# Three-column shift tiles, a new split of the weight turns, an earlier first projection tile and projection steps in the drain of an attention + feed-forward kernel

## Chip, cores, metric

One core of one Trainium2 chip. The metric is device microseconds (us) of one execution. Each kernel ran several times in turn with the kernel before ("timed"); one of these runs of each kernel was profiled and left the trace. Each kernel has one trace, so a position in a trace is one execution's.

## The reference

```
q, k, v: [8 batches, 8 heads, 576 rows, 64]    w_in: [512, 2048]   w_out: [2048, 512]
scores = q k^T / 8;  keep scores >= rowmax - tau (0.02), others get weight 0
attn   = exp(scores - rowmax) / sum;  x = attn v        # x: 4608 rows x 512
out    = (h - tanh(h)) @ w_out,  h = x @ w_in
```

## The kernel before

It works in slots: slot s does the score matmuls of query tile s+8, its own weights and the attention matmuls of tile s-2. There are 32 head pairs of 9 query tiles: 4 "A" tiles, each followed by a "B" tile of the same head, and a middle tile "M" with both heads' last 64 rows, in position 4. Four pairs are a batch. Beside attention in batch m run the hidden steps (h) of block m-1 and the projection steps (y, four quarters for each of four row tiles) of block m-2, one step being four 512-column matmuls on TensorE. VectorE makes `g` = h - tanh(h); `yo` is the copy of a finished y tile out of PSUM. The drain is what follows the slot of the last query tile.

A score tile leaves PSUM by a VectorE copy that also takes the row maximum (`sc`, `mx`). One more small VectorE operation makes the bias `nb = tau - max` of an A and a B tile together (the shift). ScalarE bends (`z`), the tile is turned (on TensorE into `psZ`, or by the DMA crossbar into `zT`), ScalarE takes exp (`pT`), TensorE multiplies with v. GpSimd splits the next pair's k and q into two fp16 parts and copies a swapped k (`kS`).

```python
def on_pe(i):                       # which tiles are turned on TensorE
    p, j = divmod(i, TPP)
    return p < HPAIR or p < 2 * HPAIR and j in (0, 1, 4, 5, 6)
...
    if kind(j) == "B":              # in scores(i)
        mx = mxs[i] = mxs.pop(i - 1)
    else:
        mx = mxs[i] = st_pool.tile([P, 2], F32, name="mx", tag="mx")
    c = int(kind(j) == "B")
    nc.vector.tensor_scalar(
        out=sc, in0=ps[:, lo : lo + S], scalar1=SC, scalar2=None,
        op0=ALU.mult, op1=ALU.max, accum_out=mx[:, c : c + 1])
...
def shift(i):                       # called one slot after scores(i)
    kd = kind(i % TPP)
    if kd == "A":
        return
    n = 2 if kd == "B" else 1
    mx = mxs.pop(i)
    nb = st_pool.tile([P, 2], F32, name="nb", tag="nb")
    nc.vector.tensor_scalar(
        out=nb[:, 0:n], in0=mx[:, 0:n], scalar1=-1.0, scalar2=tau,
        op0=ALU.mult, op1=ALU.add)
    nbs[i] = nb[:, n - 1 : n]
    if kd == "B":
        nbs[i - 1] = nb[:, 0:1]
...
EARLY = lambda m: 3 if m else 0     # quarters of y(m,0) done in the stage of h(m)
...
for s in range(-AHEAD, NTILE + LAG + 3):       # main loop, cut
    ...shift(s + 7); scores(s + 8); kink(s + 5)
    weights(s)                                  # turn on TensorE if on_pe, exp
    ...one step of todo (h or y)...
    attend(s - LAG); norm; emit_x(pair that is done)   # emit_x: psX, then VectorE copies xT, xR
    ...loads, splits (GpSimd), turns of k and q...
while stage < NMB:                  # the last two stages, after the loop
    for step in layers(stage, True): ...
```

The first h step of a stage reads all four pairs' x, the last of which `emit_x` has just turned: its fourth matmul needs VectorE's copy `xT`, and in the trace before it waited for it once from 126 to 463 us, for 0.5 us.

Of the kernel before, what the change touches and what calls it, by code (L numbers as in the profile page):

```python
# [9 lines left out]
F32 = mybir.dt.float32  # L10
# [8 lines left out]
def kernel(  # L19
# [11 lines left out]
    nc = tc.nc  # L31
# [22 lines left out]

    def on_pe(i):
        p, j = divmod(i, TPP)
        return p < HPAIR or p < 2 * HPAIR and j in (0, 1, 4, 5, 6)

    W = 2 * S

# [34 lines left out]
    for i in range(NM):  # L95
        zm = const.tile([P, 5 * P], BF16, name=f"zm{i}")
        nc.vector.memset(zm[:, S : 5 * P], -STEEP)
        zms.append(zm)


    own = const.tile([P, 2, D], BF16, name="own")
    nc.vector.memset(own, 0.0)
# [127 lines left out]

    def q_by_dma(p):

        return p >= 2 * HPAIR and p % 2 == 1

    def turn(p, t):
        hl = hls.pop((p, t))
# [52 lines left out]
    def scores(i):  # L289
        p, j = divmod(i, TPP)  # L290
        qT, kT, kS = mats[p, "q"], mats[p, "k"], mats[p, "ks"]
        ps = ps_big.tile([P, 1024], F32, name="psS", tag="big")
        main, rem, lo = slice(0, 512), slice(512, 576), 0
        if kind(j) == "B":
            main, rem, lo = slice(512, 1024), slice(448, 512), 448
        if j == 4:
            qrem = REM
            if q_by_dma(p):
                qrem = (slice(512, 640, 2), slice(513, 640, 2))
            for n, kk in enumerate((kT, kS)):  # L300
                for dst, srcs in ((main, MAIN), (rem, REM)):
                    for hh in range(2):
                        nc.tensor.matmul(  # L303
                            out=ps[64 * hh : 64 * hh + 64, dst],
                            lhsT=qT[:, qrem[hh]], rhs=kk[:, srcs[hh]],
                            start=(n == 0), stop=(n == 1),
                        )
        else:
            hh = int(j > 4)
            lhs = qT[:, j * P : (j + 1) * P]  # L310
            for n, kk in enumerate((kT, kS)):
                for dst, src in ((main, MAIN[hh]), (rem, REM[hh])):
                    nc.tensor.matmul(  # L313
                        out=ps[:, dst], lhsT=lhs, rhs=kk[:, src],
                        start=(n == 0), stop=(n == 1),
                    )
        sc = sc_pool.tile([P, S], F32, name="sc")
        if kind(j) == "B":
            mx = mxs[i] = mxs.pop(i - 1)
        else:  # L320
            mx = mxs[i] = st_pool.tile([P, 2], F32, name="mx", tag="mx")
        c = int(kind(j) == "B")
        nc.vector.tensor_scalar(  # L323
            out=sc, in0=ps[:, lo : lo + S], scalar1=SC, scalar2=None,
            op0=ALU.mult, op1=ALU.max, accum_out=mx[:, c : c + 1],
        )
        scs[i] = sc

    def shift(i):

        kd = kind(i % TPP)
        if kd == "A":
            return
        n = 2 if kd == "B" else 1
        mx = mxs.pop(i)
        nb = st_pool.tile([P, 2], F32, name="nb", tag="nb")
        nc.vector.tensor_scalar(  # L337
            out=nb[:, 0:n], in0=mx[:, 0:n], scalar1=-1.0, scalar2=tau,
            op0=ALU.mult, op1=ALU.add,
        )  # L340
        nbs[i] = nb[:, n - 1 : n]
        if kd == "B":
            nbs[i - 1] = nb[:, 0:1]

# [142 lines left out]
    def bend():  # L487
        while halves:
            m, n, ps = halves.pop(0)
            th = t_pool.tile([P, MB], F32, name="th")  # L490
            nc.scalar.activation(out=th, in_=ps, func=ACT.Tanh)  # L491
            ths.append((m, n, ps, th))

    def shrink():
        while ths:
            m, n, ps, th = ths.pop(0)
            nc.vector.scalar_tensor_tensor(  # L497
                out=gs[m][:, n, :], in0=th, scalar=-1.0, in1=ps,
                op0=ALU.mult, op1=ALU.add,
            )  # L500
# [26 lines left out]
                    )  # L527


    EARLY = lambda m: 3 if m else 0  # L530
    LAST = 1
    quarters = lambda m: [(m, ms, part) for ms in range(4) for part in range(4)]

    def layers(m, tail):


        def h_step(n):
            if tail and n % 2:
                ps = ps_big.tile([P, MB], F32, name="psHt", tag="big")
            else:  # L540
                ps = ps_h.tile([P, MB], F32, name="psH", tag="h")
            hidden(m, n, ps)

        def y_step(m, ms, part):
            if part == 0:
                odd = ms % 2
                pl, tag = (ps_o, "o") if tail and odd else (ps_y, "y")
                ys[m, ms] = pl.tile([P, d_model], F32, name="psY", tag=tag), odd
            ps, odd = ys[m, ms]
            project(m, ms, part, ps, tail and odd)  # L550

        def y_half(h):

            n = d_model // 2
            pl, tag = ((ps_y, "y"), (ps_o, "o"))[1 - h]
            ps = pl.tile([P, n], F32, name="psY", tag=tag)
            for part in range(4):
                project(m, 3, part, ps, h == 0, slice(h * n, h * n + n))

        now = quarters(m - 1)[EARLY(m - 1) :] if m > 0 else []  # L560
        if m < NMB - 1:
            now += quarters(m)[: EARLY(m)]
        else:
            now += quarters(m)[:12]
        n = 16 + len(now)


        ahead = n - max(0, EARLY(m) - 3) - LAST if m < NMB - 1 else n - 9 - LAST
        steps, at, i = [], [], 0

        def ready(y):
            last = 4 * y[2] + 3
            return y[0] < m or len(at) > last and at[last] + 2 < i

        while now or len(at) < 16:
            if len(at) < 16 and (
                not now or not ready(now[0]) or len(at) * ahead <= i * 16
            ):
                steps.append(lambda a=len(at): h_step(a))
                at.append(i)  # L580
            elif ready(now[0]):
                steps.append(lambda y=now.pop(0): y_step(*y))
            else:
                steps.append(lambda: None)
            i += 1
        if m == NMB - 1:
            steps += [lambda h=h: y_half(h) for h in range(2)]
        return steps
# [68 lines left out]
        if at < -AHEAD:  # L657
            plan.setdefault(-AHEAD, []).extend(plan.pop(at))

    kinks = {}  # L660
    for i in range(NTILE):
        kinks.setdefault(i // 2 * 2 + 2 - AHEAD if i < 4 else i - MASK, []).append(i)
    for s in range(-AHEAD, NTILE + LAG + 3):
        p, j = divmod(max(s, 0), TPP)
        if 0 <= s < NTILE and j == 2 + LAG and p % HPAIR == 0 and p >= HPAIR:
            assert not todo
            todo = layers(stage, False)
            share = len(todo) / (HPAIR * TPP - 2 - LAG)
            done, stage = 0.0, stage + 1
        if 0 <= s + AHEAD - 1 < NTILE:  # L670
            shift(s + AHEAD - 1)
        if 0 <= s + AHEAD < NTILE:
            scores(s + AHEAD)
        if s == 1 - AHEAD:
            for t in ("k", "q", "ks"):
                turn_first(t, 1)
        for i in kinks.pop(s, []):
            kink(i)
        bend()
        if 0 <= s < NTILE:  # L680
            weights(s)
            if todo:
                done += share
                if j == TPP - 1 and p % HPAIR == HPAIR - 1:
                    done = 1e9
                while todo and done >= 1:
                    todo.pop(0)()
                    done -= 1
        if s == 0:
            nc.vector.tensor_tensor(  # L690
                out=fold, in0=ident_bf[:, 0:64], in1=ident_bf[:, 64:P], op=ALU.add
            )
        shrink()
        for store in stores[:-1]:
            store()
        del stores[:-1]
        if 0 <= s - LAG < NTILE:
            attend(s - LAG)
            pp, jj = divmod(s - LAG, TPP)
            if jj == 4:  # L700
                norm(pp, 0)
            if jj == 8:
                norm(pp, 1)
        pp, jj = divmod(s - LAG, TPP)
        if jj == 1 and 0 < pp <= NPAIR:
            emit_x(pp - 1)
        for step in plan.pop(s, []):
            step()
        if True:
            if s + AHEAD in w_when:  # L710
                if loaded:
                    w_cast()
                piece = next(pieces, None)
                if piece:
                    w_load(piece)

    while stage < NMB:
        for step in layers(stage, True):
            step()
            bend()  # L720
            shrink()
            for store in stores:
                store()
            stores.clear()
        stage += 1
# [37 lines left out]
```

## Time and profile before

| | before |
|---|---|
| timed, median of 6 runs in the comparison with the change | 544.65 us (544.19 to 545.59) |
| span of the profiled run | 542.9 us |
| busy TensorE, VectorE, ScalarE, GpSimd | 93%, 82%, 81%, 54% |
| VectorE shift, two columns | 128 times, 347 ns mean |
| VectorE shift, one column (M tiles) | 32 times, 144 ns mean |
| period of a TensorE-bound stage (36 slots) | 58.26 us |

The stages have different limits, so the page's averages say little; the prediction shows the stage table. To align two kernels I read from the traces when the score copy of a given tile starts. There are 288 in each kernel, one for each tile, so the same copy marks the same slot whatever else moved: the copy of tile i belongs to slot i-8. The period is the distance of the copies of tiles 156 and 192 (and of 192 and 228).

### The profile page before, as it was taken

Reading aid. Unit: us, or ns where it says so; the run is one execution under the profiler, and the core shown is the slowest. Engines: PE = TensorE matmul, PEld = TensorE weight load, DVE = VectorE, ACT = ScalarE, POOL = GpSimd, SP = SyncE. Lnnn points to the kernel's source line nnn. Section 1 sums busy time; section 2 is a strip of 40 time slices with the busy share of each in tenths; the row PEclk is TensorE's granted clock in tenths of the full one; section 3 lists DMA queues with packets and bytes.
Section 4 is the critical chain, followed back from the end, with each engine's and each line's share of the span. In section 5 each row is a group of like instructions: output and inputs, shape, how many; then the busy total and the mean of one; then the engine's idle time right before and its main releaser. Section 6 shows DMA issues by size and latency. Waiting matters only on the chain.

```text
span 542.9 us, 12962 instructions
## 1 busy us (share of the span) xinstructions
PE 507.5 (93%) x4722; PEld 290.3 (53%) x4790; DVE 447.1 (82%) x1196; ACT 439.3 (81%) x630; POOL 290.7 (54%) x390
## 2 busy tenths in 40 slices
PE   5888888889999899999999999999999999899997
PEld 3566655555555555555555555555555555444444
DVE  4999999898888899889988989989989988544440
ACT  4899999998898888889888989899888989633330
POOL 7899987765456666557555755666655730000000
PEclk9999999998999999999999999999999999999999
DMA  7554688679697988789988999999999965310103
GB/s 211 168 182 145 205 202 175 148 131 197 141 173 160 175 169 199 163 191 195 181 188 172 177 200 186 165 171 191 192 177 179 200 127 117 83 41 39 40 39 77
DMA packets 202239, 85.13 MB, mean 157 GB/s; under 512 B 169792, under 2 KB 194624, under 8 KB 202176
## 3 DMA queue, kind: packets, MB, share of 16 engines
q1 hardware_dynamic: 201584, 83.89, 72.7%
q8 instruction: 37, 0.61, 0.5%
q10 hardware_dynamic: 592, 0.43, 0.3%
q14 instruction: 26, 0.21, 0.1%
HBM read 36.70 MB, written 9.44 MB: 85 GB/s over the span
## 4 chain that ended last, share of the span: by engine, by line
PE 67%; DVE 19%; POOL 6%; ACT 4%; issue 3%; DMA 0%; ACTq 0%; SPq 0%; DVEq 0%; POOLq 0%
PE psY L504 19%; PE psH L478 17%; PE psS L313 14%; DVE sc L323 9%; PE psO L423 5%; DVE g L497 3%; PE psS L303 3%; PE ps_k L227 3%; PE psHt L478 3%; DVE nb L337 2%; ACT z L357 2%; DVE osb L438 1%; POOL kS L256 1%; PE ps_q L227 1%; PE psO L412 1%
## 5 line engine op out<-in xcount | busy, mean ns | idle before, releaser
L323 DVE TENSOR_SCALAR_CACHE_REDUCE sc<-psS 128x576 f32<-128x576 f32 x288 | 215.3, 749 | 16.4 <-PE psS L313 11.0
L357 ACT ACTIVATE z<-sc,nb 128x576 bf16<-128x576 f32 x256 | 194.2, 771 | 21.9 <-DVE nb L337 21.3
L256 POOL COPY kS<-kT 64x1152 f16<-64x1152 f16 x62 | 70.9, 1143 | 135.8 <-DVE nb L337 133.2
L504 PE MATMUL psY<-w_out_sb,g 128*128 128x512 bf16 (+1 forms) x556 | 138.4, 373 | 2.2 <-issue 0.8
L394 ACT ACTIVATE pT<-zT 128x1152 f16<-128x1152 bf16 (+1 forms) x128 | 137.3, 1073 | 0.0
L478 PE MATMUL psH<-xT,w_in_sb 128*128 128x512 bf16 x451 | 118.0, 379 | 6.5 <-DVE g L497 4.4
L313 PE MATMUL psS<-kT,qT 128*128 128x512 f16 (+1 forms) x512 | 105.6, 288 | 11.2 <-DVE sc L323 9.2
L491 ACT ACTIVATE th<-psH 128x512 f32<-128x512 f32 x128 | 75.5, 590 | 39.2 <-PE psH L478 37.0
L313 PEld LDWEIGHTS <-qT 128*128 128x128 f16 x1024 | 73.1, 98 | 61.3 <-issue 14.5
L497 DVE SCALAR_TENSOR_TENSOR g<-th,psH 128x512 bf16<-128x512 f32 x128 | 87.2, 681 | 18.4 <-ACT th L491 18.4
L313 PE MATMUL psS<-kS,qT 128*128 128x512 f16 x496 | 101.9, 287 | 0.1
L478 PEld LDWEIGHTS <-w_in_sb 128*128 128x128 bf16 x576 | 49.4, 98 | 60.7 <-issue 7.2
L504 PEld LDWEIGHTS <-g 128*128 128x128 bf16 x592 | 51.0, 98 | 56.6 <-issue 2.9
L423 PEld LDWEIGHTS <-pT 128*128 128x128 f16 x1280 | 55.7, 98 | 25.0 <-issue 1.4
L423 PE MATMUL psO<-vb,pT 128*128 128x65 bf16 x1280 | 61.5, 194 | 0.9 <-ACT pT L394 0.6
L337 DVE TENSOR_SCALAR nb<-mx 128x2 f32<-128x2 f32 (+1 forms) x160 | 49.1, 307 | 2.5
L386 ACT ACTIVATE pT<-psZ 128x640 f16<-128x640 bf16 (+1 forms) x56 | 37.6, 671 | 5.1 <-PE psZ L377 5.0
L180 POOL TENSOR_TENSOR qhl<-qraw,qhl 128x576 f16<-128x576 f32 x31 | 39.7, 1281 | 2.6
L180 POOL TENSOR_TENSOR khl<-kraw,khl 128x576 f16<-128x576 f32 x31 | 39.7, 1281 | 2.6
L250 DVE COPY kT<-ps_k 128x1152 f16<-128x1152 f16 x31 | 23.4, 756 | 13.6 <-PE ps_k L227 13.2
L514 DVE COPY yo<-psY 128x512 f32<-128x512 f32 (+1 forms) x31 | 21.1, 679 | 11.3 <-PE psY L504 6.4
L438 DVE TENSOR_TENSOR osb<-psO,rc 128x256 bf16<-128x256 f32 x64 | 27.2, 424 | 2.2
(77 smaller groups left out, 508.4 us busy)
## 6 DMA issues: line engine op xcount, KB each, us to landing
vraw<-in_v_dram SPq DMA_DIRECT2D x32, 256.0 KB, 3.4
out_dram<-yo SPq DMA_DIRECT2D x32, 256.0 KB, 3.0
kraw<-in_k_dram SPq DMA_DIRECT2D x31, 256.0 KB, 3.2
qraw<-in_q_dram SPq DMA_DIRECT2D x31, 256.0 KB, 3.6
wt<-in_moe_w_in_dram SPq DMA_DIRECT2D x8, 512.0 KB, 4.7
wt<-in_moe_w_out_dram SPq DMA_DIRECT2D x8, 512.0 KB, 4.1
zT<-z SPq DMA_TRANSPOSE x104, 3.5
kraw<-in_k_dram SPq DMA_DIRECT2D x32, 32.0 KB, 2.8
```

The lines of the kernel that those rows point to most:

```text
L180: nc.gpsimd.tensor_tensor(out=hl[:, :, 1, :], in0=x, in1=hl[:, :, 0, :], op=ALU.subtract)
L256: nc.gpsimd.tensor_copy(out=o, in_=i)
L313: nc.tensor.matmul(out=ps[:, dst], lhsT=lhs, rhs=kk[:, src], start=(n == 0), stop=(n == 1),)
L323: nc.vector.tensor_scalar(out=sc, in0=ps[:, lo : lo + S], scalar1=SC, scalar2=None, op0=ALU.mult, op1=ALU.max, accum_out=mx[:, c : c + 1],)
L337: nc.vector.tensor_scalar(out=nb[:, 0:n], in0=mx[:, 0:n], scalar1=-1.0, scalar2=tau, op0=ALU.mult, op1=ALU.add,)
L357: nc.scalar.activation(out=z, in_=sc, func=ACT.Prelu, bias=nb, scale=1.0, alpha=STEEP)
L394: nc.scalar.activation(out=pt[:, 0 : n * P], in_=zts.pop(i)[:, 0:n, :], func=ACT.Exp)
L423: nc.tensor.matmul(out=po[:, (j - 1 - 5 * hh) + ab, :], lhsT=pt[:, blk * P : (blk + 1) * P], rhs=vb[:, hh, c, :], start=(n == 0), stop=(n ...
L478: nc.tensor.matmul(out=ps, lhsT=w_in_sb[:, c, n * P : (n + 1) * P], rhs=xs[m][:, c, :] if m < B else xR[:, c, :, :], start=(c == 0), stop= ...
L491: nc.scalar.activation(out=th, in_=ps, func=ACT.Tanh)
L497: nc.vector.scalar_tensor_tensor(out=gs[m][:, n, :], in0=th, scalar=-1.0, in1=ps, op0=ALU.mult, op1=ALU.add,)
L504: nc.tensor.matmul(out=ps, lhsT=gs[m][:, n, ms * P : (ms + 1) * P], rhs=w_out_sb[:, n, cols], start=(n == 0), stop=(n == DF_C - 1),)
```

## The change

In the trace before, a two-column shift takes 0.15 to 1.27 us. 59 of the 128 take over 0.2 us, and each of these ends 0.01 to 0.04 us after the end of an operation of GpSimd that was running. A one-column shift takes 0.14 to 0.15 us; four of the 32 lie wholly inside an operation of GpSimd (at 14.54, 25.14, 49.09 and 60.31 us). This wait of VectorE for GpSimd inside the instruction I call the lock.

The intent of the change, as I read it: three columns in the shift are an odd width, as the one column that was never held is, to keep VectorE out of the lock. Pairs 4 and 5 are turned on TensorE and 6 and 7 by the crossbar, so that the single PSUM bank `ps_y` is free for three quarters of y(0,0) in batch 1 instead of batch 2. Weights and attention of batch 0 come four slots earlier. Pair 30's q is turned by the crossbar. Three y steps run among the last attention tiles. These are the lines that matter, with others left out between them:

```diff
-        return p < HPAIR or p < 2 * HPAIR and j in (0, 1, 4, 5, 6)
+        return p < 6
+    mx3 = []
+    for i in range(6):
+        mx = const.tile([P, 3], F32, name=f"mx{i}")
+        nc.vector.memset(mx, 0.0)
+        mx3.append(mx)
-        return p >= 2 * HPAIR and p % 2 == 1
+        return p >= 2 * HPAIR and (p % 2 == 1 or p == 30)
-            mx = mxs[i] = st_pool.tile([P, 2], F32, name="mx", tag="mx")
+            mx = mxs[i] = mx3[i // 2 % len(mx3)]
-        n = 2 if kd == "B" else 1
+        n = 3 if kd == "B" else 1
-        nb = st_pool.tile([P, 2], F32, name="nb", tag="nb")
+        nb = st_pool.tile([P, 3], F32, name="nb", tag="nb")
-        nbs[i] = nb[:, n - 1 : n]
+        nbs[i] = nb[:, n // 2 : n // 2 + 1]
-    EARLY = lambda m: 3 if m else 0
+    EARLY = lambda m: 3 if m else 3
+    FIRST = 3
                 odd = ms % 2
+                odd = odd and m >= B - 1          # odd y tiles of block 6: ps_y, not ps_o
-            return y[0] < m or len(at) > last and at[last] + 2 < i
+            return y[0] < m or len(at) > (last if m else 15) and at[last] + 2 < i
-            ):
+            ) and not (m == B - 1 and i < FIRST):
+        at = i - 4 if i < HPAIR * TPP else i      # slot of weights(i); attend(i) at + LAG
+        if s == NTILE:
+            todo = layers(stage, True)            # stage 7 begins in the drain
+            share, done, stage = 1, 0.0, stage + 1
-        if 0 <= s < NTILE:
-            weights(s)
+        for i in wts.pop(s, []):
+            weights(i)
+        if 0 <= s < NTILE + FIRST:
...  (cut: attend, norm and emit_x follow the same lists; the rest of stage 7 runs after the loop)
```

More of the change, by code (lines that the diff above doesn't have):

```diff
@@ L658 @@
             plan.setdefault(-AHEAD, []).extend(plan.pop(at))
-    kinks = {}
-    for i in range(NTILE):
-        kinks.setdefault(i // 2 * 2 + 2 - AHEAD if i < 4 else i - MASK, []).append(i)
+    kinks, wts, atts = {}, {}, {}
+    for i in range(NTILE + 3):
+        at = i - 4 if i < HPAIR * TPP else i
+        atts.setdefault(at + LAG, []).append(i)
+        if i < NTILE:
+            wts.setdefault(at, []).append(i)
+            kinks.setdefault(i // 2 * 2 + 2 - AHEAD if i < 4 else i - MASK, []).append(i)
     for s in range(-AHEAD, NTILE + LAG + 3):
@@ L679 @@
         bend()
-        if 0 <= s < NTILE:
-            weights(s)
+        for i in wts.pop(s, []):
+            weights(i)
+        if 0 <= s < NTILE + FIRST:
             if todo:
                 done += share
-                if j == TPP - 1 and p % HPAIR == HPAIR - 1:
+                if s < NTILE and j == TPP - 1 and p % HPAIR == HPAIR - 1:
                     done = 1e9
@@ L696 @@
         del stores[:-1]
-        if 0 <= s - LAG < NTILE:
-            attend(s - LAG)
-            pp, jj = divmod(s - LAG, TPP)
-            if jj == 4:
-                norm(pp, 0)
-            if jj == 8:
-                norm(pp, 1)
-        pp, jj = divmod(s - LAG, TPP)
-        if jj == 1 and 0 < pp <= NPAIR:
-            emit_x(pp - 1)
+        for i in atts.pop(s, []):
+            pp, jj = divmod(i, TPP)
+            if i < NTILE:
+                attend(i)
+            if i < NTILE and jj in (4, 8):
+                norm(pp, int(jj > 4))
+            if jj == 1 and pp:
+                emit_x(pp - 1)
         for step in plan.pop(s, []):
@@ L715 @@
                     w_load(piece)
+    for step in todo:
+        step()
+        bend()
+        shrink()
+        for store in stores:
+            store()
+        stores.clear()
     while stage < NMB:
```

## The prediction

> **What bounds the kernel now.** I read the engine shares, then the 40 slices, to see that the limits differ by stage; then busy time per stage, the costliest groups, the waits and the chain stage by stage.
>
> ```profile
> PE 507.5 (93%) x4722; PEld 290.3 (53%) x4790; DVE 447.1 (82%) x1196; ACT 439.3 (81%) x630; POOL 290.7 (54%) x390
> PE   5888888889999899999999999999999999899997
> POOL 7899987765456666557555755666655730000000
> ```
>
> TensorE is busy 93% overall, but its slices start at 5 and 8, and exactly there GpSimd stands at 7 to 9. The busy times per stage (columns: window, its length, PE, PEld, DVE, ACT, POOL, clock, DMA share, GB/s) say it in numbers:
>
> ```profile
> 20.00:71.00 51.00, 44.66 (x631) 32.34 (x630) 48.43 (x136) 48.77 (x80) 48.34 (x59) 1.00 0.60 169
> 71.00:126.00 55.00, 47.88 (x542) 30.65 (x551) 51.03 (x139) 51.35 (x78) 41.53 (x51) 0.98 0.77 171
> 126.00:463.00 337.00, 328.16 (x3049) 183.60 (x3100) 303.52 (x834) 300.62 (x414) 185.00 (x237) 1.00 0.89 175
> 463.00:474.00 11.00, 9.45 (x87) 5.30 (x87) 5.88 (x15) 6.97 (x10) 0.00 (x0) 1.00 0.34 89
> ```
>
> Batch 0 (to 71 us) has VectorE, ScalarE and GpSimd all at 95% and TensorE at 88%. Batch 1 (71 to 126, the first block's hidden layer beside attention) has VectorE and ScalarE at 93%. From 126 us TensorE is at 97%, and the records show 51 fewer matmuls than weight loads, so its true idle is under 2%. In the end phase (463 to 474) it idles about 1.5 us.
>
> Which of the three engines holds batch 0? In the chain of waits between 36 and 73 us nearly every long piece is GpSimd's, and its timeline has no hole longer than 0.1 us from 16.2 to 73.3 us. Its work per head pair, from the timeline: two splits 5.2, the swapped copy of k 2.3, v 1.2, and two or three weight casts of 1.04 make 11.2 or 12.2 us. It ends a k split at 23.7, 34.9, 47.1, 58.3 and 69.6 us. TensorE turns that k at 23.8, 35.0, 47.6, 58.9, 72.5: lockstep with GpSimd up to 58.9, and then about 2.5 us later than GpSimd would allow. What delays that last pair is on VectorE:
>
> ```profile
> L337 DVE TENSOR_SCALAR nb<-mx 128x2 f32<-128x2 f32 x128 | 44.4, 347 | 2.5
> L337 DVE TENSOR_SCALAR nb<-mx 128x1 f32<-128x1 f32 x32 | 4.6, 144 | 0.0
> ...
> 63.37 1.10 DVE L337 TENSOR_SCALAR nb<-mx 128x2 f32<-128x2 f32 x1
> 65.84 1.00 DVE L337 TENSOR_SCALAR nb<-mx 128x2 f32<-128x2 f32 x1
> 68.76 0.82 DVE L337 TENSOR_SCALAR nb<-mx 128x2 f32<-128x2 f32 x1
> 71.42 0.89 DVE L337 TENSOR_SCALAR nb<-mx 128x2 f32<-128x2 f32 x1
> ```
>
> The same operation on one column never takes over 0.15 us; on two it takes 0.14 to 1.27, and about one microsecond where GpSimd is busy. So the two-column form waits inside the instruction for GpSimd.
>
> [...] 347 against 144 ns, with the long ones beside GpSimd's 1.14 to 1.29 us operations. [...] nothing in this trace has an odd width above one, so it cannot decide. [...] four 512-column matmuls start 0.865 us after the last four throughout the tail.
>
> **The change, part by part.**
>
> 1. *Odd-width shift.* 128 two-column operations become three-column ones on preset tiles. If the lock goes, the mean falls from 347 towards 165 ns (the unblocked ones), 128 × 0.18 = 23 us of VectorE time. Little of it is on the path. Batch 0: the last pair no longer lags GpSimd, 2.9 us (72.5 less 69.6), and a blocked 0.63 us operation at 13.2 us, ahead of the first long GpSimd run, gives 0.4: **3.3 us**; the rest is capped by GpSimd's contiguous work. Batch 1: 16 operations averaging 424 ns hold 4.2 us of stall; part 2 says what remains of that. From 126 us on TensorE waits 3.0 us for g and 1.6 us for sc; a faster VectorE may return **1.0**. The sum if the lock goes is in the last paragraph of this part.
>
> 2. *Pairs 4 and 5 on TensorE, 6 and 7 by crossbar; three quarters of the first projection tile in batch 1.* Tiles turned on TensorE fall from 56 to 54 (8 added, 10 removed); exp time is even (577+695 ns against 1,152 for a tile couple, four couples each way). The purpose is the bank: y(0,0) holds the single y bank, which the turned weights also use, so they must be through before it begins. Projection steps of batch 2 fall from 19 to 16, 3 × 0.865 = **2.6 us** off a TensorE-bound stage. Batch 1 has room: 48 of 55 us. But the 16 hidden steps are now spread over 21 positions instead of 16, so over some 24 slots instead of 32. Per slot while pairs 4 and 5 run, TensorE has scores 0.53, attention 0.17, k and q turns 0.14 with the x turn, weight turns 0.26, hidden 0.66 × 0.865 = 0.57: 1.67 us, against ScalarE 1.55 and VectorE 1.55 (1.67 with stalls). For 14 slots TensorE sets 23.4 us; for 11 slots about 1.57 each, 17.3; for the last 11, without hidden steps, 1.25 each, 13.7: 54.4, and 3% of loose ends make 56 us, against 57.4 now (71.5 to 128.9): **1.4** saved if the lock goes, and nothing (57.6) if it stays.
>
> 3. *Weights of batch 0 four steps earlier.* They fill ScalarE's idle time before 19 us (waits of 1.0, 1.45 and 0.8 us there) and leave a hole at slots 32 to 35. The stage that follows starts at the same slot, and GpSimd's list is the same: **0**.
>
> 4. *Pair 30's q by crossbar.* Nine turns off a saturated TensorE (about 0.5 us for nine in the steady stage) and one 0.75 us VectorE copy: **0.5**.
>
> 5. *Three projection steps in the drain.* TensorE now idles 0.57 us for exp and 0.74 us for the normalization; three steps of 0.865 cover both, but y(6,1) now needs the bank that y(6,0) leaves, with a 0.69 us copy between, and nothing beside it: 1.5 less 0.8, **0.7**.
>
> If the lock goes: 3.3 + 1.4 + 1.0 + 2.6 + 0.5 + 0.7 = 9.5, so 535 us. If it stays: 2.6 + 0.5 + 0.7, with about 0.3 for the ramp, 4.1, so 540.3 us.
>
> **The rivals.** *(A) The lock stays at three columns.* [...] Against: someone built preset three-column tiles for this, and one column never blocks. 540.3 us. *(B) VectorE is relieved, but GpSimd takes over more fully than I allow:* its contiguous run already reaches 73.3 us, and k and q splits were met within 0.5 us by TensorE. Then batch 0 gives 1 to 2 instead of 3.3, and the total is about 537. *(C) The crowded first half of batch 1 gives back what the y steps gain:* TensorE at 1.67 us a slot, with psZ in one bank, and q of pair 9, for which TensorE already waits for a DMA of the transposing kind:
>
> ```profile
> 122.11 0.42 PE L313 MATMUL psS<-kT,qT 128*128 128x512 f16 x2 [1.46 <-DMA qT<-qhl]
> 124.33 0.64 PE L313 MATMUL psS<-kT,qT 128*128 128x512 f16 x2 [0.75 <-DVE sc L323]
> ```
>
> After that wait matmuls run about 1.6 times as long until 127 us (granted clock 0.83 in 120 to 130). More crossbar turns stand in that queue now; if the wait doubles, 1.5 us are lost, and if it goes, 2 us are won. *(D) Everything overlaps better than I sum:* with VectorE free, batch 1 becomes ScalarE's 51.5 us (its work in 71.5 to 128.9), and up to 3 us more come off: 532.
>
> **Range and chances.** I give the lock's going 0.62[...]. Then 535 with about 2 us either way; else 540.3 with 1.5. The point between, nearer the likelier branch, is 536.5 us. A range of 532.5 to 541 takes in both centres. Faster by over 2% means under 533.5 us, which needs the lock gone and (D): 0.62 × 0.27, some 0.17. Slower than 2% would need a stall of 15 us, and nothing points there: 0.01.
>
> **What would show each step.** Part 1: the three-column group at 140 to 180 ns mean with a maximum under 0.3 us, VectorE's total near 425 us; a mean still over 300 shows (A). GpSimd still without holes to about 70 us, and TensorE's waits for its splits above the 2.7 us of now, show that it caps batch 0. Part 2: first hidden step at about 68 us (71.5 now), first psY about 10 us before the next stage, weight turns ended before it, and a step of batch 2 shortened. Part 3: exp beginning near 14 us instead of 19, no earlier hidden step from it. Part 4: 18 whole-width q copies instead of 19. Part 5: psY matmuls between the last attention matmuls, with one wait for a yo copy. The prediction is wrong if batch 0 ends well before 67 us (GpSimd was no cap), if batch 1 takes over 58 us (crowding), or if the TensorE-bound stages change their period of 58.3 us by more than the 1 us in all that I allow.

## The result, and the profile after

Timed: 544.0 us (543.29 to 544.87, 6 runs) against 544.65 us (544.19 to 545.59, 6 runs). The ratio is 0.9987, 95% interval 0.9972 to 1.0001: the same. (Ratios are the mean time of one kernel's runs over that of the other's of the same rounds, so not quite the ratio of the medians.) The forecast was 536.5 us, with 532.5 to 541 as its range; the result lies above it. The profiled spans are 542.9 and 541.5 us.

First the groups of instructions on VectorE, after (count, then busy us and mean ns):

```profile
L343 DVE TENSOR_SCALAR nb<-mx 128x3 f32<-128x3 f32 x128 | 41.0, 320 | 2.3
L343 DVE TENSOR_SCALAR nb<-mx 128x1 f32<-128x1 f32 x32 | 4.6, 144 | 0.0
```

Three columns still block: 320 ns against 347, and the longest takes 1.24 us. The busy time per stage, after, in the same windows as in the prediction:

```profile
20.00:71.00 51.00, 45.73 (x618) 31.81 (x618) 48.35 (x140) 48.20 (x79) 48.33 (x60) 1.00 0.59 185
71.00:126.00 55.00, 49.50 (x532) 30.55 (x537) 49.42 (x138) 50.37 (x75) 40.49 (x51) 1.00 0.80 162
126.00:463.00 337.00, 325.54 (x3039) 181.96 (x3089) 303.69 (x833) 302.05 (x416) 185.95 (x237) 1.00 0.88 177
463.00:474.00 11.00, 10.11 (x79) 5.15 (x79) 5.36 (x14) 4.82 (x8) 0.00 (x0) 1.00 0.28 76
```

TensorE does more in the first two stages and the drain, and less from 126 us on, where it was the bound. The slot marks show by how much each stage moved (lengths in us, from the starts of the score copies of tiles 48, 84, 120, 264, 287 and the end of the span):

| stretch | before | after | moved | predicted, lock stays |
|---|---|---|---|---|
| to slot 40 (batch 0) | 70.64 | 68.63 | -2.0 | -0.3 |
| slots 40 to 76 (batch 1) | 56.93 | 57.47 | +0.5 | 0 |
| slots 76 to 112 (batch 2) | 61.74 | 58.83 | -2.9 | -2.6 |
| slots 112 to 256 (four stages) | 233.00 | 235.30 | +2.3 | 0 |
| slots 256 to 279 | 38.03 | 37.93 | -0.1 | -0.5 |
| last score copy to the end | 82.61 | 83.34 | +0.7 | -0.7 |

So 4.4 us were won by slot 112, and 3.0 of them given back: 0.57 us in each of the four equal stages, whose period went from 58.26 to 58.83 us, and 0.7 in the drain. Of the 0.57 us, 0.5 sit in one slot (from the score copy of tile 190 to that of 191: 0.89 us before, 1.38 after). Here are VectorE and GpSimd at the start of such a stage, before (timeline: start, us, engine, line, operation):

```profile
303.75 0.75 DVE L323 TENSOR_SCALAR_CACHE_REDUCE sc<-psS 128x576 f32<-128x576 f32 x1
304.54 0.17 DVE L337 TENSOR_SCALAR nb<-mx 128x2 f32<-128x2 f32 x1
304.64 0.76 DVE L323 TENSOR_SCALAR_CACHE_REDUCE sc<-psS 128x576 f32<-128x576 f32 x1
305.32 0.42 DVE L468 COPY xT<-psX 128x512 bf16<-128x512 bf16 x1
...
303.86 0.67 POOL L176 TENSOR_SCALAR qraw<-qraw 128x576 f32<-128x576 f32 x1
304.60 0.67 POOL L179 CAST qhl<-qraw 128x576 f16<-128x576 f32 x1
```

and the same slot after:

```profile
300.04 0.75 DVE L329 TENSOR_SCALAR_CACHE_REDUCE sc<-psS 128x576 f32<-128x576 f32 x1
300.83 0.68 DVE L343 TENSOR_SCALAR nb<-mx 128x3 f32<-128x3 f32 x1
301.42 0.74 DVE L329 TENSOR_SCALAR_CACHE_REDUCE sc<-psS 128x576 f32<-128x576 f32 x1
302.10 0.41 DVE L474 COPY xT<-psX 128x512 bf16<-128x512 bf16 x1
...
300.08 0.68 POOL L182 TENSOR_SCALAR qraw<-qraw 128x576 f32<-128x576 f32 x1
300.82 0.66 POOL L185 CAST qhl<-qraw 128x576 f16<-128x576 f32 x1
```

Before, the shift starts 0.79 us and GpSimd's cast 0.85 us after the score copy: the shift is first and takes 0.17 us. After, the cast starts at 0.78 us, just ahead of the shift, and the shift lasts 0.68 us, to the cast's end. All that follows on VectorE comes half a microsecond later, the copy of xT too, for which a hidden step waits. TensorE's waits from 126 to 463 us (total us, times, longest), before and then after:

```profile
PE psH L478 <- DVE xT L468: 0.5, 1, 0.5
```

```profile
PE psH L484 <- DVE xT L474: 2.1, 5, 0.4
```

Why does the cast come earlier? Six slots earlier stand the middle tile's shift and the next score copy, and after a cut the shift after that; first before, then after:

```profile
297.23 0.14 DVE L337 TENSOR_SCALAR nb<-mx 128x1 f32<-128x1 f32 x1
297.29 0.75 DVE L323 TENSOR_SCALAR_CACHE_REDUCE sc<-psS 128x576 f32<-128x576 f32 x1
...
300.17 0.30 DVE L337 TENSOR_SCALAR nb<-mx 128x2 f32<-128x2 f32 x1
```

```profile
293.43 0.14 DVE L343 TENSOR_SCALAR nb<-mx 128x1 f32<-128x1 f32 x1
293.70 0.76 DVE L329 TENSOR_SCALAR_CACHE_REDUCE sc<-psS 128x576 f32<-128x576 f32 x1
...
296.59 0.17 DVE L343 TENSOR_SCALAR nb<-mx 128x3 f32<-128x3 f32 x1
```

The score copy starts 0.06 us after the shift before the change and 0.27 us after it with the change. In the code, `i // 2` is the same number for the M tile (j = 4) and the next A tile (j = 5) of an even pair, so both use one preset tile, and the A tile's maximum must not be written before M's shift has read it. GpSimd's run, which begins with the swapped copy right after that shift, does not wait. Of VectorE's 0.21 us, 0.13 are regained at the last line of each fence: before, that shift was held by a v cast of GpSimd (0.30 us), now it is not (0.17 us), and GpSimd's next cast is held for 0.03 us instead. What is left is the 0.07 us by which the q cast comes earlier against the score copy. That is the theory that the experiments test.

### The profile page after: what moved, and what is told of

Its sections match the earlier page's. It is cut to its first block, busy times and chain, and to the rows that moved or that the text cites. A ratio compares the mean times of both kernels' runs of the same rounds, so it can differ in the third digit from the quotient of the medians.

```text
span 541.5 us, 12959 instructions
## 1 busy us (share of the span) xinstructions
PE 506.7 (94%) x4704; PEld 288.0 (53%) x4771; DVE 445.9 (82%) x1203; ACT 438.3 (81%) x628; POOL 291.1 (54%) x390
## 4 chain that ended last, share of the span: by engine, by line
PE 62%; DVE 24%; issue 5%; ACT 5%; DMA 3%; SPq 0%; DVEq 0%; ACTq 0%; POOL 0%
PE psY L510 18%; PE psH L484 16%; PE psS L319 13%; DVE sc L329 12%; PE psO L429 4%; DVE g L503 4%; PE psS L309 3%; PE ps_k L233 2%; PE psHt L484 2%; ACT pT L392 2%; ACT z L363 2%; DVE yo L520 2%; DMA qT<-qhl 2%; DVE nb L343 2%; DVE kT L256 1%
## 5 line engine op out<-in xcount | busy, mean ns | idle before, releaser
L400 ACT ACTIVATE pT<-zT 128x1152 f16<-128x1152 bf16 (+1 forms) x130 | 139.1, 1070 | 0.0
L484 PE MATMUL psH<-xT,w_in_sb 128*128 128x512 bf16 x455 | 119.2, 379 | 7.2 <-DVE g L503 3.9
L343 DVE TENSOR_SCALAR nb<-mx 128x3 f32<-128x3 f32 (+1 forms) x160 | 45.6, 285 | 2.3
L392 ACT ACTIVATE pT<-psZ 128x640 f16<-128x640 bf16 (+1 forms) x54 | 35.4, 658 | 5.2 <-PE psZ L383 4.8
L520 DVE COPY yo<-psY 128x512 f32<-128x512 f32 (+1 forms) x33 | 22.5, 681 | 12.2 <-PE psY L510 7.6
```

Source lines behind the costliest of these rows:

```text
L343: nc.vector.tensor_scalar(out=nb[:, 0:n], in0=mx[:, 0:n], scalar1=-1.0, scalar2=tau, op0=ALU.mult, op1=ALU.add,)
L400: nc.scalar.activation(out=pt[:, 0 : n * P], in_=zts.pop(i)[:, 0:n, :], func=ACT.Exp)
L484: nc.tensor.matmul(out=ps, lhsT=w_in_sb[:, c, n * P : (n + 1) * P], rhs=xs[m][:, c, :] if m < B else xR[:, c, :, :], start=(c == 0), stop= ...
```

## Experiments

Each was timed beside the kernel before on the same chip: e1 to e4 on one, e5 to e8 on another, e9 to e12 on a third, e13 on a fourth. Only ratios are compared across chips. "Period" is that of the TensorE-bound stages, read from the trace.

| run | what | median us | ratio to before (95%) | period us |
|---|---|---|---|---|
| the change | | 544.0 | 0.9987 (0.9972 to 1.0001) | 58.83 |
| e1_before_odd | before + three-column shift | 552.62 | 1.0111 (1.0084 to 1.0138) | 58.82 in the profile |
| e2_after_two | change with two columns | 541.05 | 0.9915 (0.9902 to 0.9928) | 58.27 |
| e3_after_split | change, one-column shifts | 538.45 | 0.9871 (0.9858 to 0.9883) | 57.92 |
| e4_before_split | before, one-column shifts | 538.79 | 0.9877 (0.9863 to 0.9891) | 57.86 to 58.17 |
| e5_after_owntile | change, tiles not shared | 541.41 | 0.9925 (0.9912 to 0.9937) | 58.25 to 58.50 |
| e6_after_nudge | change + fill ahead of the k split | 544.81 | 0.9985 (0.9971 to 0.9998) | 58.93 to 59.15 |
| e7_split_late_w | e3 without early weights | 538.69 | 0.9880 (0.9865 to 0.9895) | 57.91 |
| e8_split_old_drain | e3 with the old drain | 537.11 | 0.9851 (0.9837 to 0.9864) | 57.91 |
| e9_after_nudge_q | change + fill ahead of the q split | 546.46 | 1.0022 (0.9979 to 1.0065) | 60.19 in the profile |
| e10_before_early_w | before + early weights | 544.03 | 0.9972 (0.9960 to 0.9985) | 58.25 |
| e11_split_first1 | e8 + one step in the drain | 536.99 | 0.9843 (0.9829 to 0.9856) | 57.91 |
| e12_split_no_q30 | e8 without pair 30's crossbar | 537.27 | 0.9844 (0.9830 to 0.9857) | 57.91 |
| e13_shared_split | e3 with the shared tiles | 538.13 | 0.9881 (0.9863 to 0.9899) | 57.95 |

All gave correct results.

### e1_before_odd: the odd width alone

The `mx3`, `n = 3` and `nb` lines of the diff above, put into the kernel before; nothing else.

> Kernel before with the three-column shift alone. Theory 1 (the lock stays at an odd width, and only the moments at which it strikes move): the three-column group keeps a mean of 300 to 360 ns with a maximum over 1.1 us, VectorE's busy time within 5 us of 447, the time within 0.4% of before, either way. Theory 2 (three columns or the preset tiles cost something of their own in the TensorE-bound stages): the period of a stage rises from 58.26 to about 58.8 us, and the time by 2 to 3 us. Theory of the change (odd width frees the lock): mean 140 to 180 ns, 540 us or less.

The three-column group means 353 ns, with the longest at 1.27 us: the lock stays, and the change's reason for the odd width falls. The profiled run has the period 58.82, like the change. But only that run took 547.36 us; the five others took 552.3 to 552.9. The time was thus worse than any theory had it. What made those five slower has no trace of its own; e9 below shows a second pattern, with a period of 60.19, and 4 stages of 1.36 us more would be 5.4 us, which fits 547.4 + 5.4.

### e2_after_two: the change without it

```diff
-            mx = mxs[i] = mx3[i // 2 % len(mx3)]
+            mx = mxs[i] = st_pool.tile([P, 2], F32, name="mx", tag="mx")
-        n = 3 if kd == "B" else 1
+        n = 2 if kd == "B" else 1
```

> Changed kernel with the shift at two columns again. Theory 1: the group means 300 to 350 ns as with three, the stage period is 58.26 or 58.83 according to where the block falls, the time 541 to 544.5 us. Theory 2 (the odd width itself costs 0.57 us a stage): period back to 58.26 and 541.5 us. Theory 3 (another part of the change costs the 0.57 us): period stays at 58.83 and the time at 544.

Period back to 58.27, 541.05 us. So the rest of the change is worth 0.85%, and the three columns with their tiles take most of it back. This does not yet tell three columns from the shared tile.

### e3_after_split and e4_before_split: no lock at all

```diff
-        nc.vector.tensor_scalar(
-            out=nb[:, 0:n], in0=mx[:, 0:n], scalar1=-1.0, scalar2=tau, ...)
+        for c in range(n):
+            nc.vector.tensor_scalar(
+                out=nb[:, c : c + 1], in0=mx[:, c : c + 1], scalar1=-1.0,
+                scalar2=tau, ...)
```

> Changed kernel with two one-column operations in place of each three-column one. One column never blocked in either trace (144 ns). Theory 1: no shift over 0.2 us; the hidden step at a stage's start no longer waits for the copy of xT beyond the 0.1 us of before, so the period is 58.3 us or less (2.3 us over four stages), and batch 0 and 1 lose the remaining 4.5 and 1.9 us of blocked VectorE time as far as it is on the path: 537 to 541 us. If the lock is not what costs (theory 3): 543 to 545[...].

> Kernel before with two one-column operations in place of each two-column one. By the prediction's working (its terms for the lock: 3.3 in batch 0, 1.4 in batch 1, 1.0 later) some 5.7 us come off: 538.5 to 541. If GpSimd caps batch 0 more fully than that (rival B): 541.5 to 543.5. If the lock is no matter: 544 to 546, for the 128 added operations.

The group on VectorE in e3:

```profile
L338 DVE TENSOR_SCALAR nb<-mx 128x1 f32<-128x1 f32 x288 | 35.4, 148 | 0.0
```

More instructions, and less time: 288 of 148 ns, none over 0.16 us, in place of 160 that held VectorE for 45.6 us. Both kernels gain, the change 1.16 points on what it had (0.9987 to 0.9871), the kernel before 1.23%. The prediction's terms for the lock summed to 5.7 us; e4 shows 545.7 - 538.79 = 6.9. In its trace slot 40 comes at 67.64 instead of 70.64 us, 3.0 where 3.3 were predicted; but 1.3 of these lie before the score copy of tile 9, where kernels with the same code so far differ by 1.0 us (e3, e8, e11 and e12 below: 19.1 to 20.1 us). From tile 9's copy to slot 40 it is 49.05 against 50.79 us, 1.7. GpSimd's timeline still has no hole over 0.15 us from 14 to 72 us. With the lock gone, the whole rest of the change (e3 against e4) is worth nothing clear of noise; without its drain steps (e8, on another chip) it is worth 0.26 points.

### e5_after_owntile: three columns, but no shared tile

```diff
-            mx = mxs[i] = mx3[i // 2 % len(mx3)]
+            mx = mxs[i] = mx3[(5 * p + (j + 1) // 2) % len(mx3)]
```

> Changed kernel, still three columns, but each maximum gets a preset tile of its own: in the changed kernel the tile of the middle query tile and of the next one are the same in every even pair, so that the score copy of the next waits for the shift of the middle one (0.27 us from shift to score copy there, 0.06 without). Theory A (the sharing moves VectorE by 0.21 us against GpSimd, and so lets a q cast of GpSimd begin just ahead of one shift, which then blocks for half a microsecond in front of the copy of xT): stage period 58.26 us, that shift 0.17 instead of 0.68 us, time about 541. Theory B (three columns as such cost it): period 58.83, time 543.3 to 545. The group's mean stays about 300 ns in both.

The score copy after M's shift starts 0.07 us after it again, the cast comes at 0.83 us instead of 0.78, the shift at 0.79 takes 0.17 us, and the period is 58.25 (58.50 in the last of three stages). 541.41 us, or 0.9925 of the kernel before: two columns had 0.9915. So the width itself does neither good nor harm that can be seen; the sharing costs 0.6% (0.9987 against 0.9925).

### e6_after_nudge and e9_after_nudge_q: move GpSimd by a tenth of a microsecond

```diff
         hl = hl_pool.tile([P, TPP, 2, D], FP16, name=f"{t}hl", tag=t)
+        if t == "k":            # e6;  in e9: if t == "q"
+            nc.gpsimd.memset(nudge, 0.0)      # [128, 2]
```

> Changed kernel with one tiny GpSimd fill of two columns ahead of each k split, so that GpSimd's run comes some 0.06 to 0.1 us later against VectorE. Theory A: the shift falls into the gap between two GpSimd operations again, 0.17 instead of 0.68 us, and the period goes to about 58.3 us though VectorE's wait for the shared tile (0.21 us) stays; 541 to 542.5. Theory B, or a theory in which the wait itself costs the 0.57: period stays at 58.8, 543.5 to 545.

A miss in its direction: the cast came earlier, at 0.70 us. Just ahead of the k split, a v cast and a shift were due at the same moment. In the change the shift won; here the cast did, and the shift took 0.31 instead of 0.17 us. That moved VectorE back by 0.14 us and the fill GpSimd by only some 0.07 (in e9's trace such a fill takes 0.10 us, and the split after it starts 0.07 us after the fill's start). The shift was then held 0.60 instead of 0.68 us: its end follows the cast's end (0.70 + 0.66 = 1.36 against 0.79 + 0.60 = 1.39). The period rose to 58.93 us.

> The nudge of e6 came out the wrong way: with the fill before the k split GpSimd skipped a wait and the q cast began at 0.70 instead of 0.78 us after the score copy, and the shift at 0.79 was held until the cast's end again (0.60 instead of 0.68 us). Here the 0.1 us fill stands before the q split alone, so the cast comes at about 0.88 us, after the shift has begun. Theory A (it is the order of these two that costs): that shift back to about 0.17 us, stage period 58.3 to 58.4 us in place of 58.83, no wait of the hidden step for xT, 541 to 542, though the shared tile and its 0.21 us wait stay. Theory that the wait itself costs the 0.57 us: period 58.8 and 543.5 to 545.

A second miss, through the same tie of a v cast of GpSimd and a shift (0.79 us after the score copy). In the change the shift won, took 0.17 us, and GpSimd's cast 0.32; in e9's profiled run the shift took 0.32 and the cast 0.29, and GpSimd ran 0.18 us earlier from there on. Its k split now began 0.07 us ahead of the next shift (e9's VectorE and GpSimd timelines):

```profile
302.11 1.27 DVE L346 TENSOR_SCALAR nb<-mx 128x3 f32<-128x3 f32 x1
305.27 0.84 DVE L346 TENSOR_SCALAR nb<-mx 128x3 f32<-128x3 f32 x1
...
302.04 1.28 POOL L189 TENSOR_TENSOR khl<-kraw,khl 128x576 f16<-128x576 f32 x1
304.80 1.28 POOL L189 TENSOR_TENSOR qhl<-qraw,qhl 128x576 f16<-128x576 f32 x1
```

The first shift waits out the whole split, and the period is 60.19 us, with the same code on VectorE and the same wait for the shared tile as in the change. The timed runs of this one kernel are 543.93, 544.77, 548.14 and 550.6 us: more than one pattern occurs, so its ratio says little, and I draw on the trace alone. Both misses speak for the lock, and neither shows the cost going away; that e5 and e13 do.

### e13_shared_split: keep the sharing, take the lock away

e3, but with the `mx3[i // 2 % 6]` tiles of the change.

> The changed kernel with its preset, partly shared tiles, but one-column shifts. Theory A (the wait for the shared tile costs only through the lock): the 0.2 us gap between the middle tile's shift and the next score copy stays in every even pair, yet the stage period is 57.9 to 58.0 us, as without sharing (57.92), and the time 538 to 539. Theory that the wait itself costs 0.5 us a stage: period 58.4 to 58.5 and 540.5.

The score copy still starts 0.2 us late in even pairs (that slot lasts 2.80 us, 2.59 without sharing), and the period is 57.95 against 57.92. The wait itself is worth 0.03 us a stage. With e5 this settles it: the sharing costs only because it makes a shift run into GpSimd's cast.

### e10_before_early_w and e7_split_late_w: the early weights

e10: the three lists of the change (`kinks, wts, atts`) in the kernel before. e7: `at = i` in e3.

> Kernel before with the early weights of batch 0 alone, two-column shifts. The changed kernel reached slot 40 2.0 us earlier than before with the lock in place, which the prediction had put at 0.3. Theory A (the early weights did that: the four slots without weights near the end of batch 0 leave VectorE's blocked shifts less to hold up): slot 40 at 68.6 to 69.2 against 70.6, time 543 to 544. Rival (chance of where the locks fall): slot 40 at 70 or later, time 544.5 or more.

Slot 40 at 68.27 us instead of 70.64, and 0.28% faster in time: the 2.0 us of batch 0 come from this part. Most of it is not kept: batch 1 takes 58.84 instead of 56.93 us, so slot 76 is only 0.5 us ahead, and the profiled spans differ by 0.9 us. What batch 1 waited for was not followed up.

> The changed kernel with one-column shifts (538.45 us before), and batch 0's weights at their old slots. In the kernel before with one-column shifts batch 0 reached slot 40 at 67.6 us, with the early weights at 69.1, where TensorE waits 5.0 us in all for z. Theory A (early weights cost batch 0 about 1.5 us when the lock is gone): slot 40 at 67.6, time 536.5 to 537.5. Rival (it is another part that costs, such as more turns in batch 1): slot 40 stays at 69.1 and the time at 538.5.

Slot 40 at 68.83 against 69.12, and the ratio 0.9880 against 0.9871: no difference. With the lock in place the early weights help a little, without it no help can be seen in the time. My theory that they cost 1.5 us then was wrong: e3, e8, e11 and e12 have the same code up to slot 40 and reach it at 68.16 to 69.12 us, and counted from tile 9's copy e3 takes 49.06 us, e7 49.69 and e4 49.05.

### e8_split_old_drain, e11_split_first1, e12_split_no_q30: the small parts

```diff
-    FIRST = 3
+    FIRST = 0                       # e8, e12;  e11: 1
-                odd = odd and m >= B - 1
-        return p >= 2 * HPAIR and (p % 2 == 1 or p == 30)      # e12 only
+        return p >= 2 * HPAIR and p % 2 == 1
```

> The changed kernel with one-column shifts, and the drain of before (no projection steps among the last attention tiles, odd y tiles in the attention's bank). In the traces from slot 279's score copy to the end: 82.6 us before, 83.3 changed. Theory A (the drain's steps cost, since y(6,1) waits 0.78 us for the bank of y(6,0) and later y tiles 0.28 us each): 0.7 us faster, 537.7. Prediction's part 5: 0.7 us slower, 539.1.

From the last score copy to the end: 82.67 us, and 83.36 in e3. Three steps in the drain, with the change of banks that goes with them, cost 0.7 us. TensorE in the drain, before and then after:

```profile
470.79 0.49 PE L423 MATMUL psO<-vb,pT 128*128 128x65 bf16 x10 [0.57 <-ACT pT L394]
472.02 0.40 PE L455 MATMUL psX<-ident_bf,osb 128*128 128x128 bf16 x4 [0.74 <-DVE osb L438]
```

```profile
469.70 1.02 PE L510 MATMUL psY<-w_out_sb,g 128*128 128x512 bf16 x4 [0.78 <-DVE yo L520]
470.87 1.02 PE L510 MATMUL psY<-w_out_sb,g 128*128 128x512 bf16 x4
471.77 0.40 PE L461 MATMUL psX<-ident_bf,osb 128*128 128x128 bf16 x4
```

The two waits went (1.31 us), and a wait of 0.78 us for the bank came; three later row tiles wait for the same bank, the first of them here, after the change:

```profile
477.25 1.03 PE L510 MATMUL psY<-w_out_sb,g 128*128 128x512 bf16 x4
479.42 1.02 PE L510 MATMUL psY<-w_out_sb,g 128*128 128x512 bf16 x4 [0.28 <-DVE yo L520]
```

The other two start at 486.77 and 494.12 us. The trace marks 0.28 us of wait each, but from one y step to the next it is 2.17 us there and 1.73 elsewhere: 0.44 each, 1.3 in all. So 1.3 us won, 0.8 and 1.3 lost make -0.8, near the measured -0.7. That is the term that I had left out.

> The changed kernel with one-column shifts, the old banks for the odd y tiles, and one projection step (y(6,0), last quarter) instead of three among the last attention tiles; 537.11 us with none, 538.45 with three. It covers the 0.57 us wait for exp and takes no bank that another tile holds: 536.5 if the waits for banks were what made the three cost; 537.1 or more if the drain has other limits.

82.21 us from the last score copy, against e8's 82.67: one step, with the old banks, wins 0.46 us in the trace; the times (0.9843 against 0.9851) don't tell it from none.

> As e8 (one-column shifts, old drain, 537.11 us), but pair 30's q turned on TensorE as before. Prediction's part 4: 0.5 us slower, 537.6. If the 0.6 us that the crossbar gives is given back by TensorE's wait for that transfer (0.38 us seen in the changed kernel) and by a hidden step behind it: 537.1.

No difference (0.9844 against 0.9851): pair 30's turn by the crossbar gains nothing that can be seen in the time. In the trace before, its nine turns on TensorE take 0.65 us, from 427.93 us to the next matmul at 428.58. In the change's trace TensorE waits 0.38 us for that q's transfer.

## Why the prediction was wrong, point by point

Two steps failed. Part 1's first step, that the lock goes: it stays at three columns (320 ns mean, where 140 to 180 were to show its going). And the sum for the case that it stays (4.1 us off, 540.3 us; measured 544.0): it had no cost for the new tiles of the shift, which took 2.3 us in the four equal stages and 0.6 in batch 2, and it had the drain's steps as 0.7 us won, which were 0.7 lost.

1. **The choice between the branches.** I gave the lock's going 0.62, because someone had built tiles for it; the trace before has no shift of an odd width above one, so it could not show which. The group's mean of 320 ns and e1 show that it stays. Rival (A) was right in mechanism; its 540.3 us was also near what the change does with two columns (541.05, e2). This choice put the centre of the forecast 4 us too low.

2. **"If the TensorE-bound stages change their period ... by more than the 1 us in all".** This sign of being wrong came true (2.3 us), and the step behind it failed even in the branch where the lock stays: I took the odd width for neutral where it does not help. It came with shared tiles; they hold VectorE for 0.21 us, of which 0.07 are left against GpSimd six slots later, one shift runs into a cast, and 0.57 us are lost four times (2.3 us), besides 0.6 in batch 2 (58.83 against 58.22 in e2). e5 removes the sharing and gets it back, e13 keeps it and removes the lock.

3. **The value of the lock** (3.3 + 1.4 + 1.0 = 5.7 us) came out near in the sum, 6.9 in e4, but not in its parts, so some of that is luck. In e4's trace it is 3.0 to slot 40 (1.7 without the start of the run), 0.65 in batch 1 and 2.8 after it (1.6 in batch 2, 1.2 in the four equal stages). Part 1 took the last pair's lag of 2.9 us off whole; in e4 it still is 1.8 (its k split ends at 68.67 us, its turn starts at 70.51), so for batch 0 rival (B) was the nearer. In the equal stages the lock costs 0.35 us even in the good pattern (58.26 against 57.91); there TensorE's waits for `g` fell, as part 1 had it, from 3.0 us before to 1.9 in e3 (126 to 463 us). The wait for xT that the change's pattern adds I had not seen.

4. **Part 2**, 2.6 us off batch 2 and nothing on batch 1: measured -2.9 and +0.5. Right in mechanism; that the number fits is partly luck, as the -2.9 holds the 0.6 us lost to the shared tiles (e2 has 58.22, -3.5). With the lock gone batch 2 falls from 60.15 (e4) to 57.86 to 58.88 (e3, e7, e8, e11, e12), 1.3 to 2.3. Batch 1 takes 57.47 with the lock (forecast 57.6) and 56.2 without (e3, e8; forecast 56), so neither the crowding of rival (C) nor the 51.5 of rival (D) came.

5. **Part 3**, "0": it gave 2.0 us by slot 40 with the lock in place (e10 alone: 2.4, of which 0.9 are left in the span; 0.28% of the time), and nothing seen in the time without (e7). I had called GpSimd the cap of batch 0, but in its last ten slots VectorE's blocked shifts set the pace, as the prediction itself said; fewer of them were blocked (12 in place of 14 from 20 to 71 us, 4.5 instead of 6.0 us). Why the slots without weights lead to that was not tested.

6. **Part 5**, 0.7 us won: 0.7 us lost. The bank wait at the first step was foreseen (0.8 us, measured 0.78), the three later ones, 1.3 us together, were not. The 1.5 us to be won was the idle time of the whole window; the two waits that it named sum to 1.31.

7. **Part 4**, 0.5 us: nothing measurable.

8. **A slip that moved nothing:** the items of GpSimd's work per pair sum to 10.8 or 11.8 us; the 11.2 or 12.2 are the distances of its k splits, gaps between operations included.

Together: 4.4 us won by slot 112 (4.1 had been the whole sum of this branch), then 2.3 us and 0.7 us given back. 1.4 us are left between the two profiled spans, and 0.65 between the medians.

The version to keep is e11 or e8: the change with one-column shifts and without the three drain steps, 537 us, about 1.5% faster than the kernel before and 1.4% than the change.

## What to carry to other kernels

Here the lock cost by where it struck, not by its sum: some 23 us of blocked VectorE time (the prediction's estimate, 128 × 0.18 us) were worth 6.9 us (e4), and one shift held for 0.5 us in front of the copy that starts a stage decided over 2.3. The two engines ran in a fixed rhythm, and a wait of 0.21 us elsewhere moved one past the other, so compare the period of a stage, and where in it the loss sits, before blaming the edited line. If a trace shows a small operation held by another engine inside the instruction, as the shift was at two and at three columns (347 and 320 ns mean), look for a form that the trace shows is not held (here one column: 288 operations of 148 ns mean, none over 0.16 us). And give buffers that follow each other different tiles (the shared ones cost 0.6% here, e5).
